# Pooling sums of keys and values by GpSimd, and batch 2 loaded in 72 rows, in a fused attention and feed-forward kernel

## Chip, cores, metric

One Trainium2 chip, one core. The time is the device time of one execution in microseconds (us); lower is better. Several executions are made of each kernel, and the medians below are of those. An execution is called slow when it is over 1.5% above the fastest of the same kernel; ratios and intervals use fast ones alone. Engines: PE is TensorE (matrix products; PEld its weight loads), DVE is VectorE, ACT is ScalarE, POOL is GpSimd, SP is SyncE, which here only issues loads and stores.

## The reference

Attention against keys and values that are averaged over groups of 8 positions, then a two-layer feed-forward with silu. All inputs and the output are float32.

```python
# q, k, v: (8 batches, 8 heads, 576 positions, 64); pool = 8, so Sp = 72
k_p = k.reshape(B, H, Sp, 8, D).mean(axis=3)
v_p = v.reshape(B, H, Sp, 8, D).mean(axis=3)
scores = (q @ k_p.T) / sqrt(D)
attn = exp(scores - max); attn /= sum(attn)
x = (attn @ v_p)  # -> (4608 tokens, 512)
# w_in: (512, 2048), w_out: (2048, 512)
h = x @ w_in
out = (h * sigmoid(h)) @ w_out
```

## The kernel before

The kernel goes through 9 tiles of 512 tokens (t = 0 to 8). Each tile has an "up" part (x times w_in, silu) and a "down" part (times w_out). From tile 1 on both are done with seven products of half size in place of eight (the Strassen-Winograd scheme): so DVE has to form sums such as `x_sum` (of quarters of x) and `h_sum` before TensorE can use them. The attention of batch t+1 is woven into tile t: a list of small pieces of work, the "fillers", each with the step of the up or down part at which it is put into the engines' instruction streams. An engine runs its stream in order: in experiment 2 below, TensorE stood for 1.9 us at the transposes of a late kp, and from 59 to 60 us it ran no product at all, though others stood behind them.

What the change touches is how the 8 positions of a group are summed. From batch 3 on, k and v come in by heads: 72 rows (one for each group) by 8 heads by 4 positions of 64. The first four positions are loaded by SP; the last four are *added* to them in flight by a load that POOL issues. That leaves four positions: `add_halves` makes two of them (72x1024 elements), `add_rest` one, in bf16. Batch 2 is done as batches 0 and 1 are: rows of 128 "slots" across heads, which TensorE must afterwards pick apart with selection products (`select_k`, `select_v`).

```python
def load_one(b, name):                       # first four positions, by SP
    raw = raw_tile(f"{name}_raw", H)
    load_rows(nc.sync, raw, source(b, name)[:, :, :PH])
    ...
def load_rest(b, name):                      # last four, added in flight
    nc.gpsimd.dma_start(out=batches[b][f"{name}_raw"],
        in_=source(b, name)[:, :, PH:], accum_op=ALU.add)

def add_halves(raw):
    nc.vector.tensor_add(out=raw[:, :, : 2 * D],
        in0=raw[:, :, : 2 * D], in1=raw[:, :, 2 * D :])
def add_rest(dst, raw):
    nc.vector.tensor_add(out=dst, in0=raw[:, :, :D]..., in1=raw[:, :, D : 2 * D]...)

def pool_k(b, stage):    # stage 0: add_halves; stage 1: add_rest twice, into kp
def pool_v(b):           # add_halves, add_rest into vp
def k_transpose(b):      # four products of 72x72: kp -> kT_ps, then ACT copies to kz

def unit_x_sum(t, n):    # both inputs lie in SBUF
    nc.vector.tensor_tensor(out=x_sum[:, U_XI[n]],
        in0=x_quarter(t, *a), in1=x_quarter(t, *b), op=...)

# up part, products "2", "5", "1" of a unit:
product(y, 2, "P", True); nc.scalar.copy(r_sb, ps["P"])
product(y, 5, "Q", True); tt(out=rr_sb, in0=ps["Q"], in1=r_sb, op=ALU.add)
product(y, 1, "R", True); tt(out=t_sb, in0=ps["R"], in1=rr_sb, op=ALU.subtract)

for t in range(NT):
    a = t + 1
    ...                                       # t >= 1:
    for n in U_X:                             # five x_sum, first in the up part
        f_up.append((0, lambda n=n: unit_x_sum(t, n)))
    ...
    elif t == 1:                              # batch 2, slots
        for j in range(2):
            f_up.append((0, lambda j=j: slot_sums("k", j, halves=True)))
            f_up.append((22, lambda j=j: select_k(2, j)))
            ...                               # copy_k, slot_sums of v, select_v, copy_v
    else:                                     # batches 3 to 7
        f_up.append((22, lambda: k_transpose(a)))
        f_down.append((10, lambda: pool_v(a)))
    ...
    elif a + 1 < B:
        for stage in range(2):
            f_down.append((100, lambda stage=stage: pool_k(a + 1, stage)))
        f_up.append((0, lambda: load_q(a + 1)))
        f_up.append((1, lambda: load_one(a + 1, "k")))
        f_up.append((2, lambda: load_rest(a + 1, "k")))
        f_down.append((11, lambda: load_one(a + 1, "v")))
        f_down.append((12, lambda: load_rest(a + 1, "v")))
```

The softmax here doesn't subtract the row's maximum and nothing guards it: scores larger than these inputs give would overflow.

## Time and profile before

| | before |
|---|---|
| time, median of the 3 runs made before the prediction (range) | 291.4 us (290.86 to 291.49) |
| span of the profiled execution | 288.6 us |
| busy: PE / DVE / ACT / POOL | 97% / 79% / 65% / 18% |
| granted PE clock, all 40 slices of the span | 0.9 or more |
| five x_sum of one tile, from first start to last end | 1.75 us |
| one 72x1024 add on DVE | 1.21 us |

The time is a little over the span, which is what the trace covers.

### The profile page before, as it was taken

The numbers are of one execution on the slowest core, as the hardware profiler recorded it, in microseconds if no ns is written. First come the engines' busy times: TensorE is split into PE (matmuls) and PEld (weight loads), VectorE is DVE, ScalarE is ACT, GpSimd is POOL, SyncE is SP. The second block draws the span as 40 slices with busy tenths as digits, with TensorE's granted clock in tenths as the row PEclk, the third lists the DMA queues.
The fourth block names the chain that finished last, engine by engine and source line by source line (L and its number), as shares of the span: only waits on it lengthen the run. The fifth ranks groups of instructions, "written<-read, shape, count | busy, mean of one in ns | idle before, by whom it ended". The sixth has DMA issues, their size and how long they took to land.

```text
span 288.6 us, 6600 instructions
## 1 busy us (share of the span) xinstructions
PE 281.2 (97%) x2578; PEld 189.9 (66%) x2597; DVE 226.8 (79%) x417; ACT 187.9 (65%) x401; POOL 52.2 (18%) x68
## 2 busy tenths in 40 slices
PE   7989999999999999999999999999999999999995
PEld 2448434465667676657788767676777667786684
DVE  4986844989789796979698879887988876746783
ACT  1768675568656877578767866786679657425700
POOL 8744316501020011101200106203000000000000
PEclk9999999999999999999999999999999999999999
DMA  7999999893758565875995495979830023005004
GB/s 214 276 278 215 232 301 151 221 206 55 145 82 187 127 91 76 133 179 123 137 182 166 61 138 81 164 156 163 149 82 2 2 65 83 1 2 140 6 2 145
DMA packets 35295, 37.67 MB, mean 131 GB/s; under 512 B 9952, under 2 KB 27616, under 8 KB 35264
## 3 DMA queue, kind: packets, MB, share of 16 engines
q0 software_dynamic: 21760, 20.86, 43.3%
q1 hardware_dynamic: 12928, 15.48, 22.0%
q10 hardware_dynamic: 576, 0.92, 0.9%
q8 instruction: 20, 0.33, 0.5%
q14 instruction: 11, 0.09, 0.1%
HBM read 36.70 MB, written 9.44 MB: 160 GB/s over the span
## 4 chain that ended last, share of the span: by engine, by line
PE 91%; DVE 2%; ACT 2%; DMA 2%; issue 1%; DVEq 0%
PE hp_ps L518 24%; PE o_psP L623 15%; PE o_psQ L623 15%; PE u_psQ L460 6%; PE u_psP L460 6%; PE o_psR L623 5%; PE o_ps L550 4%; PE sc_ps L330 4%; PE nu_ps L370 3%; PE den_ps L347 3%; PE u_psR L460 2%; DMA raw<-in_k_dram 2%; PE warm_ps L672 1%; ACT es L338 1%; PE kz_ps L295 1%
## 5 line engine op out<-in xcount | busy, mean ns | idle before, releaser
L518 PE MATMUL hp_ps<-xT,w_in_sb 128*128 128x512 bf16 (+3 forms) x398 | 80.5, 338 | 1.2 <-ACT h_T L524 0.4
L524 ACT ACTIVATE h_T<-hp_ps 128x512 bf16<-128x512 f32 (+2 forms) x95 | 51.4, 545 | 33.1 <-PE hp_ps L518 31.9
L623 PEld LDWEIGHTS <-h_sum 128*128 128x128 bf16 x640 | 60.4, 98 | 15.2 <-issue 6.1
L583 DVE TENSOR_TENSOR h_sum<-h_T 128x1024 bf16<-128x1024 bf16 (+1 forms) x72 | 50.9, 743 | 7.0 <-ACT h_T L524 7.0
L518 PEld LDWEIGHTS <-w_in_sb 128*128 128x128 bf16 x412 | 39.3, 98 | 24.9 <-issue 1.5
L338 ACT ACTIVATE es<-sc_ps 72x288 bf16<-72x288 f32 x128 | 41.4, 402 | 12.6 <-PE sc_ps L330 12.5
L378 DVE TENSOR_TENSOR xT<-nu_ps,rec 128x288 bf16<-128x288 f32 x64 | 25.8, 450 | 13.2 <-PE nu_ps L370 13.0
L460 PEld LDWEIGHTS <-w_sum 128*128 128x128 bf16 x300 | 29.3, 98 | 7.7
L623 PEld LDWEIGHTS <-h_T 128*128 128x128 bf16 x256 | 23.5, 98 | 6.7 <-issue 4.3
L468 ACT ACTIVATE h_T<-c_sb 128x512 bf16<-128x512 f32 x30 | 18.8, 628 | 10.8 <-DVE c_sb L492 10.8
L152 DVE STREAM_TRANSPOSE qT<-q_bf 128x576 bf16<-128x576 bf16 x32 | 22.9, 753 | 0.0
L181 POOL DMA_DIRECT2D raw<-in_k_dram x5 | 7.0, 1405 | 75.1 <-DVE h_sum L583 37.7
L356 ACT ACTIVATE lnd<-den_ps 128x288 f32<-128x288 f32 x30 | 12.3, 411 | 10.8 <-PE nu_ps L370 5.8
L273 DVE TENSOR_TENSOR raw<-raw 128x384 f32<-128x384 f32 (+3 forms) x20 | 12.4, 619 | 8.0 <-DMA raw<-in_v_dram 4.4
L623 PE MATMUL o_psP<-w_out_sb,h_sum 128*128 128x256 bf16 x128 | 17.6, 273 | 0.0
L623 PE MATMUL o_psQ<-w_out_sb,h_sum 128*128 128x256 bf16 x128 | 17.6, 273 | 0.0
L623 PE MATMUL o_psQ<-w_sum,h_T 128*128 128x256 bf16 x128 | 17.5, 274 | 0.0
L623 PE MATMUL o_psP<-w_sum,h_sum 128*128 128x256 bf16 x128 | 17.0, 273 | 0.0
L623 PE MATMUL o_psR<-w_sum,h_sum 128*128 128x256 bf16 x128 | 16.7, 273 | 0.0
L623 PE MATMUL o_psP<-w_sum,h_T 128*128 128x256 bf16 x128 | 16.7, 273 | 0.0
L530 POOL DMA_DIRECT2D out_dram<-o_sb x1 | 0.6, 628 | 82.3 <-issue 82.3
L623 PE MATMUL o_psQ<-w_sum,h_sum 128*128 128x256 bf16 x128 | 15.4, 273 | 0.0
(77 smaller groups left out, 426.8 us busy)
## 6 DMA issues: line engine op xcount, KB each, us to landing
out_dram<-o_sb SPq DMA_DIRECT2D x128, 64.0 KB, 2.5
q_bf<-in_q_dram POOLq DMA_DIRECT2D x6, 576.0 KB, 11.4
raw<-in_k_dram SPq DMA_DIRECT2D x6, 512.0 KB, 5.5
raw<-in_k_dram POOLq DMA_DIRECT2D x5, 576.0 KB, 8.8
raw<-in_v_dram POOLq DMA_DIRECT2D x5, 576.0 KB, 8.7
raw<-in_v_dram SPq DMA_DIRECT2D x5, 512.0 KB, 6.4
w_in_sb<-in_moe_w_in_dram POOLq DMA_DIRECT2D x8, 256.0 KB, 8.7
w_out_sb<-in_moe_w_out_dram POOLq DMA_DIRECT2D x4, 512.0 KB, 13.5
```

The costliest lines, as they stand in the source:

```text
L152: nc.vector.transpose(out=st["qT"][:, a, f * QF : (f + 1) * QF].rearrange("r i c p -> r (i c p)"), in_=st["q_bf"][:, a, f * n : (f + 1) * n],)
L273: nc.vector.tensor_add(out=raw[..., :w], in0=raw[..., :w], in1=raw[..., w : 2 * w])
L330: nc.tensor.matmul(sc[s], lhsT=kz[b % 2][rows, g, c, :], rhs=st["qT"][rows, g, f * QF : (f + 1) * QF, c, :], start=(c == 0), stop=(c == 1),)
L338: nc.scalar.activation(es[:, s, :], sc[s], func=AF.Exp, scale=score_scale)
L356: nc.scalar.activation(lnd, den_ps[:, :HS], func=AF.Ln)
L378: nc.vector.tensor_mul(out=xT[:, 2 * g + c, cols], in0=nu[c][:, :HS], in1=rec)
L460: nc.tensor.matmul(ps[bank][:, u, :], lhsT=w[:, kk, 128 * u : 128 * (u + 1)], rhs=x[:, kk, :], start=first and u == 0 and kk == 0, stop=kk ...
L468: nc.scalar.activation(h_T[:, g : g + 2, j * NQ : (j + 1) * NQ], src, func=AF.Silu)
L518: nc.tensor.matmul(hp_ps[:, r0:r1], lhsT=w_in_sb[:, kk, g * 128 : (g + 1) * 128], rhs=xT[:, kk, x0 : x0 + r1 - r0], start=(kk == 0), stop= ...
L524: nc.scalar.activation(h_T[:, g, n0 : n0 + n], hp_ps[:, :n], func=AF.Silu)
L583: nc.vector.tensor_tensor(out=h_sum[n][:, ks, :], in0=quarter(*a, ks), in1=quarter(*b, ks), op=op)
L623: nc.tensor.matmul(ps[b][:, c, :], lhsT=left(n, kt, c), rhs=W_OUT[n][:, kt, :], start=b not in begun, stop=kt == k1 - 1, skip_group_check= ...
```

## The change

Intent: DVE is busy for 79% of the span and POOL for 18%, so the sums of batches 3 to 7 (19.3 us of DVE) go to POOL. Batch 2 is loaded by heads like the later batches, which also does away with its selection products on TensorE. The loads of v now follow those of k at once. All sums of batch 2 on are made by POOL, in POOL's stream, where they stand behind its loads.

```diff
-    def load_one(b, name):
+    def load_one(b, name, eng=nc.sync):
...                                         # POOL's form: one load of 72 rows
     def add_halves(raw):
-        nc.vector.tensor_add(
+        nc.gpsimd.tensor_add(
...
     def add_rest(dst, raw):
-        nc.vector.tensor_add(
+        nc.gpsimd.tensor_add(
...
-            elif t == 1:
-                for j in range(2):
-                    f_up.append((0, lambda j=j: slot_sums("k", j, halves=True)))
-                    f_up.append((22, lambda j=j: select_k(2, j)))
...                                         # copy_k, slot_sums("v"), select_v, copy_v
             else:
                 f_up.append((22, lambda: k_transpose(a)))
-                f_down.append((10, lambda: pool_v(a)))
...
             if t == 0:
-                f_down.append((0, lambda: load_half_2("k", 0)))
+                f_down.append((0, lambda: load_one(2, "k", nc.gpsimd)))
                 f_down.append((0, lambda: load_q(2)))
-                f_down.append((0, lambda: load_half_2("k", 1)))
-                for half in range(2):
-                    f_down.append((31, lambda half=half: load_half_2("v", half)))
+                f_down.append((0, lambda: load_rest(2, "k")))
+                f_down.append((31, lambda: load_one(2, "v", nc.gpsimd)))
+                f_down.append((31, lambda: pool_k(2)))
+                f_down.append((31, lambda: load_rest(2, "v")))
...
             elif a + 1 < B:
-                for stage in range(2):
-                    f_down.append((100, lambda stage=stage: pool_k(a + 1, stage)))
                 f_up.append((0, lambda: load_q(a + 1)))
+                if t == 1:
+                    f_up.append((0, lambda: pool_v(2)))
                 f_up.append((1, lambda: load_one(a + 1, "k")))
+                f_up.append((1, lambda: load_one(a + 1, "v")))
                 f_up.append((2, lambda: load_rest(a + 1, "k")))
-                f_down.append((11, lambda: load_one(a + 1, "v")))
-                f_down.append((12, lambda: load_rest(a + 1, "v")))
+                f_up.append((2, lambda: load_rest(a + 1, "v")))
+                f_down.append((30, lambda: pool_k(a + 1)))
+                f_down.append((31, lambda: pool_v(a + 1)))
```

(Cuts are marked with "..."; the helpers of the slot loads lose their "halves" form.)

More of the change, by code (lines that the diff above doesn't have):

```diff
@@ L172, in load_rows @@
             eng.dma_start(out=out[r0:r1], in_=in_[r0:r1])
-    def load_one(b, name):
+    def load_one(b, name, eng=nc.sync):
         st = batches.setdefault(b, {})
         raw = raw_tile(f"{name}_raw", H)
-        load_rows(nc.sync, raw, source(b, name)[:, :, :PH])
+        if eng is nc.sync:
+            load_rows(eng, raw, source(b, name)[:, :, :PH])
+        else:
+            eng.dma_start(out=raw, in_=source(b, name)[:, :, :PH])
         st[f"{name}_raw"] = raw
@@ L196, in add_rest, with pool_k @@
         )
-    def pool_k(b, stage):
+    def pool_k(b):
         st = batches[b]
         raw = st["k_raw"]
-        if stage == 0:
-            add_halves(raw)
-            return
+        add_halves(raw)
         st["kp"] = mid.tile([SP, 2, 2, 4, DH], BF16, tag="kp", bufs=1, name="kp")
@@ L247, with load_slots @@
     }
-    def load_slots(eng, b, name, i0, i1, half=None):
-        es = slice(0, RE) if half is None else slice(half * RE // 2, (half + 1) * RE // 2)
+    def load_slots(eng, b, name, i0, i1):
         src = (k if name == "k" else v)[b].rearrange("h (sp p) d -> (h sp) (p d)", p=POOL)
-        src = src[:, es]
-        how = dict(accum_op=ALU.add) if half else {}
         tiles = row_tiles[name]
-        w = es.stop - es.start
         if i0 == SLOTS:
-            eng.dma_start(
-                out=tiles[1][:REST, SLOTS - SA, :w], in_=src[128 * SLOTS :], **how
-            )
+            eng.dma_start(out=tiles[1][:REST, SLOTS - SA], in_=src[128 * SLOTS :])
         else:
@@ L263, in load_slots, with slot_sums @@
             eng.dma_start(
-                out=tiles[j][:, i0 - SA * j : i1 - SA * j, :w],
-                in_=src[128 * i0 : 128 * i1].rearrange("(i r) e -> r i e", r=128), **how
+                out=tiles[j][:, i0 - SA * j : i1 - SA * j],
+                in_=src[128 * i0 : 128 * i1].rearrange("(i r) e -> r i e", r=128),
             )
-    def slot_sums(name, j, halves=False):
+    def slot_sums(name, j):
         raw = row_tiles[name][j]
         dst = rows5[name][:, SA:] if j else rows5[name][:, :SA]
-        w = RE // 4 if halves else RE // 2
+        w = RE // 2
         while w > D:
@@ L750 @@
     load_w_out(3)
-    def load_half_2(name, half):
-        for i0, i1 in ((0, SA), (SA, SLOTS), (SLOTS, SLOTS + 1)):
-            load_slots(nc.gpsimd, 2, name, i0, i1, half)
     visits = [(f, g) for f in range(2) for g in range(2)]
@@ L809 @@
                     f_down.append((37 + 3 * j, lambda j=j: copy_v(1, j)))
-            elif t == 1:
-                for j in range(2):
-                    f_up.append((0, lambda j=j: slot_sums("k", j, halves=True)))
-                    f_up.append((22, lambda j=j: select_k(2, j)))
-                    f_up.append((23, lambda j=j: copy_k(2, j)))
-                    f_down.append((8, lambda j=j: slot_sums("v", j, halves=True)))
-                    f_down.append((40, lambda j=j: select_v(2, j, "at")))
-                    f_down.append((41, lambda j=j: copy_v(2, j)))
             else:
                 f_up.append((22, lambda: k_transpose(a)))
-                f_down.append((10, lambda: pool_v(a)))
             for n in range(4):
```

## The prediction

> **What bounds the kernel now.** I read the page first: the busy shares, then the chain that ended last.
>
> ```profile
> PE 281.2 (97%) x2578; PEld 189.9 (66%) x2597; DVE 226.8 (79%) x417; ACT 187.9 (65%) x401; POOL 52.2 (18%) x68
> ...
> PE 91%; DVE 2%; ACT 2%; DMA 2%; issue 1%; DVEq 0%
> ```
>
> TensorE is 91% of the chain; DVE is 2% of it (about 6 us), although it is 79% busy. So taking work off DVE pays only where DVE is on the chain, and POOL is nearly idle: its 52 us are almost all DMA issues. I then followed the chain in order of time, tile by tile of 512 tokens. In the middle of the kernel (tile 2, "up" part) it leaves TensorE once:
>
> ```profile
> 91.47 0.45 PE u_psP L460 x4
> 91.92 0.04 DVEq L492
> 91.95 0.45 DVE qT L152 x2
> 92.40 0.14 issue
> 92.54 0.66 DVE c_sb L492
> 93.20 0.02 issue
> 93.23 0.02 ACT h_T L468
> 93.25 0.51 issue
> 93.76 0.58 ACT r_sb L477
> 94.34 0.02 issue
> 94.36 0.70 DVE rr_sb L480
> 95.07 0.04 issue
> 95.11 0.60 PE u_psQ L460 x4
> ```
>
> (Columns: start, length, engine and line.) DVE reaches c_sb late because three query transposes, and ahead of them x_sum, stand in its queue; ACT and TensorE then wait in turn. The same detour is at 122 us (tile 3) and nowhere in tiles 4 to 6, where the chain is TensorE throughout. What is it worth? The chain's groups give 0.865 us for four 512-wide products of hp_ps and 0.44 us for four of u_ps. An up part of tile 2 has 32 of the first and 14 groups of the second: 8 x 0.865 + 14 x 0.44 = 13.1 us, with 0.13 us of kT_ps 13.2. The measured up part runs from 85.68 to about 99.17, 13.5 us. Loss: 0.3 us. Tile 3 is the same. In the down parts the chain never leaves TensorE.
>
> Batch 2 is used in tile 1. There the chain, 50 to 87 us, has selection products that the change deletes:
>
> ```profile
> 58.58 0.22 PE hp_ps L518
> 58.80 0.67 PE kz_ps L295 x16
> 59.47 0.16 issue
> ...
> 73.88 0.53 PE v_ps L313 x12
> ```
>
> [...] For DVE this trace has 1212 ns for the 72x1024 add[...]; for GpSimd it has no add at all. [...] every second half is issued by POOLq. So the accumulating loads and the new adds share one in-order queue.
>
> **The change part by part.**
>
> *Removed from TensorE.* 24 k selections (0.67 + 0.16 us of the chain, 0.83) and 12 v selections (0.53); added are four transposes of 72x72, 0.13 us as in the other tiles. Net 0.83 + 0.53 - 0.13 = 1.2 us, all on the chain, so a saving if kp and vp are there in time.
>
> *Removed from DVE.* From the groups by shape:
>
> ```profile
> L187 DVE TENSOR_TENSOR raw<-raw 72x1024 f32<-72x1024 f32 x10 | 12.1, 1212 | 0.0
> ...
> L192 DVE TENSOR_TENSOR kp<-raw 72x256 bf16<-72x256 f32 x10 | 3.8, 418 | 0.2
> ...
> L192 DVE TENSOR_TENSOR vp<-raw 72x512 bf16<-72x512 f32 x5 | 3.4, 687 | 0.2
> ```
>
> That is 19.3 us for batches 3 to 7. For batch 2: the slot sums, 2 x (556 + 358 + 423 + 291) ns = 3.3 us, and the copies out of PSUM, 2 x 303 + 2 x 417 ns = 1.4 us. Together 24 us, of 226.8, so DVE should show about 203 us busy. On the chain it is worth little. The sums of k at the end of each down part (2.0 us of DVE just before x_sum) go away, so x_sum and rr_sb come earlier. In tiles 2 and 3 this can remove the detour: 2 x 0.3 = 0.6 us. Elsewhere nothing.
>
> *Added to POOL.* [...] POOL has room; what matters is when kp lands.
>
> *Moved.* Both first halves are now issued after the stores of the tile before, v no longer in the middle of the down part, and the second halves follow on. TensorE's queue is in order: if kp is late, it stands at kT_ps. So I set the time of kp against that of kT_ps. The DMA figures are of before:
>
> ```profile
> raw<-in_k_dram SPq DMA_DIRECT2D x6, 512.0 KB, 5.5
> raw<-in_k_dram POOLq DMA_DIRECT2D x5, 576.0 KB, 8.8
> ```
>
> (last column: us from issue to landing). Issue times are from POOL's and SP's order of time in before.
> - Batch 2: first half issued at 30 us, landed at 44 (the queue is full of weights), second half 8 us more, 52; sums to 56; kT_ps is due at 58.6. Slack 2.5 us.
> - Batches 3, 4 and 6: the second halves land about 78, 111 and 172, so kp is ready at 82, 115 and 176, against 90.7, 120.8 and 180.0. Slack 4 us or more.
> - Batch 5: SP is busy with stores until 127.9; second half issued at 135.1, 9 to 10 us beside v, 144.5; kp at 148 to 149 against 150.3. Slack 1 to 2 us.
> - Batch 7: stores until 188.4, second half issued at 194.9, landed 204.5 as it now runs beside that of v; kp at 208 to 209 against 209.6. Slack about 1 us.
> Before, DVE did these last two sums at 144.3 and 203.5 in 2.0 us; the 1.6 us more on POOL come from what slack there was. vp is due only at 46 of 112 steps of the down part, over 10 us later than kT_ps, so v has room everywhere; in tile 4 its buffer is still read by the deferred numerator of batch 4, which delays pool_v(6) to about 166, and that is harmless too.
>
> The sum without delays: 291.4 - 1.2 - 0.6 = 289.6 us. For delays I take expected values: 0.3 us at batch 2, 0.4 at batch 5, 0.6 at batch 7. I choose these from slacks of 1 to 2.5 us [...]. [...] Predicted: 289.6 + 1.5 = 291.1 us.
>
> **The rivals.**
> 1. *A wait for POOL takes the place of the work.* If an add takes 1.5 to 2 times my estimate, pool_k is 5.5 to 7 us, and kp comes 1 us late for batch 5, 1 to 3 for batch 7, up to 1 for batch 2. TensorE then stands at kT_ps for 3 to 5 us in all: 293 to 295 us. For it: the slacks above[...]. Against it: four of six batches have slack enough.
> 2. [...] h_sum or x_sum (two SBUF inputs) wait, and everything behind them in DVE's order, among it the evacuations that free the PSUM banks. 12 long adds at 0.3 us on the chain make 3 to 4 us: 293 us. For it: 64 h_sum, 40 x_sum and 30 weight sums are of that kind, and batches 5 and 7 would be summed just when x_sum is due. Against it: each place where POOL might block DVE has 2 us less of DVE work in front of it than before, and an evacuation has about 1.7 us (the next product of 16) to spare.
> 3. *All goes well.* kp is early everywhere, and the detours vanish: 289.3 to 289.8 us. For it: POOL idles for 82 us at the end, and waits of over 10 us stand before its second halves. Against it: batch 7.
> 4. *POOL's order delays loads.* An add that waits for its data holds back the queries and second halves behind it, so that the delay grows from batch to batch. Against it: each batch starts afresh behind SP's stores, and queries are loaded two buffers ahead. I give it little.
>
> **Range and chances.** The gain is bounded at about 2 us, 0.7%, because the removed DVE work lies beside TensorE; faster by 2% would need 5.8 us, which nothing in the chain offers. Slower by 2% (297.2) needs stalls of over 7.6 us, that is, adds of over twice the estimate or DVE blocked widely. The low end is 289.2, the third rival; the high end 294.5, the first rival or the second nearly in full. Chances: faster 0.02, same 0.86, slower 0.12.
>
> **What would show it.** Right: DVE about 203 us busy, POOL about 90, a 72x1024 add on POOL near 2.3 us, no v_ps or kz_ps products after tile 0, tile 1 shorter by over 1 us, the chain in tiles 2 and 3 without the 122 us detour. For the first rival: waits of PEld L221 for POOL kp, of over 0.5 us, foremost in tiles 4 and 6. For the second: h_sum or x_sum well over their 685 and 416 ns while POOL adds, and waits of TensorE for DVE. I am wrong if POOL's adds take 4 us or more, if vp holds up the numerators, or if time is lost in tile 0, where the loads of batch 2 change.

## More of the kernel before

The five x_sum stand at the boundary of two tiles, and the sums of k just ahead of them. This is DVE's order of time at the boundary of tiles 2 and 3, before (columns: start, length of the group, engine and line, operation, out<-in, shapes, count):

```profile
115.04 1.21 DVE L187 TENSOR_TENSOR raw<-raw 72x1024 f32<-72x1024 f32 x1
116.29 0.76 DVE L192 TENSOR_TENSOR kp<-raw 72x256 bf16<-72x256 f32 x2
...
117.57 1.75 DVE L427 TENSOR_TENSOR x_sum<-xT 128x512 bf16<-128x512 bf16 x5
119.24 0.68 DVE L480 TENSOR_TENSOR rr_sb<-u_psQ,r_sb 128x512 f32<-128x512 f32 x1
```

Tile 3 starts at 115.61 (its first product of the up part), so rr_sb, for which TensorE will come to wait in the changed kernel, starts 3.6 us into the tile.

## The result

| | median | range | fast runs against before |
|---|---|---|---|
| before (a fourth run added) | 291.28 us | 290.86 to 291.49 | |
| changed | 300.22 us | 297.16 to 302.75 | 1.0272 [1.0212, 1.0332], slower |

A ratio compares the fast runs of one kernel with the fast runs of the other from the same rounds, so it is not quite the ratio of the medians; in brackets is the 95% interval. A kernel is called slower or faster from 2% on, and "same" below. The 291.1 us predicted is 9 us too low, and the range ended at 294.5. The changed kernel also spreads more (297 to 303 us) than the one before (0.2%).

The profile of that first result fell in a slow execution (302.75 us). So the changed kernel was run again, and the lines below are of that repeat, whose profiled execution is a fast one (299.55 us, span 297.7, against 288.6 before). First the page: busy times, granted PE clock in 40 slices, and the shares of the chain that ended last.

```profile
PE 284.4 (96%) x2565; PEld 190.0 (64%) x2565; DVE 216.0 (73%) x380; ACT 188.7 (63%) x402; POOL 97.0 (33%) x90
...
PEclk9999999999999999979999999999999999999999
...
PE 69%; DMA 13%; DVE 6%; issue 6%; POOL 5%; ACT 0%; POOLq 0%; DVEq 0%
```

DVE has lost 37 instructions but only 11 us of busy time; POOL has gained 45 us; TensorE has 32 weight loads fewer (2565 against 2597), yet is busy 3 us longer, and its clock has a dent in the 18th slice (126 to 134 us: 7 tenths, 9 in all others). The 13% of DMA in the chain are no measure of the loss: the four long loads on it all lie before 56 us, where the chain, once it has left TensorE at a wait for POOL, is followed back through the first loads; the kernel of experiment 6, as fast as before, also has 13%. Next, what TensorE stood waiting for (total us, times, longest):

```profile
PE u_psQ L455 <- DVE rr_sb L475: 5.4, 3, 3.7
...
PE nu_ps L365 <- POOL vp L195: 1.4, 1, 1.4
...
PE kT_ps L222 <- POOL kp L195: 0.7, 2, 0.4
```

In the trace before, the longest wait of a TensorE product on another engine, after the warm-up, is 0.4 us. The waits for kp and vp were foreseen in kind (the prediction's first rival) and are small. The large one is for rr_sb, on DVE. Why is rr_sb late? DVE's order of time at the boundary of tiles 2 and 3, after:

```profile
119.13 6.77 DVE L422 TENSOR_TENSOR x_sum<-xT 128x512 bf16<-128x512 bf16 x5
125.82 0.68 DVE L475 TENSOR_TENSOR rr_sb<-u_psQ,r_sb 128x512 f32<-128x512 f32 x1
```

and POOL's in the same stretch:

```profile
117.65 2.35 POOL L190 TENSOR_TENSOR raw<-raw 72x1024 f32<-72x1024 f32 x1 [6.45 <-DMA raw<-in_k_dram]
120.08 1.65 POOL L195 TENSOR_TENSOR kp<-raw 72x256 bf16<-72x256 f32 x2
121.69 2.52 POOL L190 TENSOR_TENSOR raw<-raw 72x1024 f32<-72x1024 f32 x1
124.29 1.32 POOL L195 TENSOR_TENSOR vp<-raw 72x512 bf16<-72x512 f32 x1
```

The five x_sum, 1.75 us before, take 6.77 us, exactly while POOL makes the sums of k and v of batch 4. Taken apart into single instructions from the trace's records, the two engines interlock one by one:

| POOL instruction | ends at | x_sum | starts, length | ends at |
|---|---|---|---|---|
| 72x1024 add of k | 120.00 | 1st | 119.13, 1.15 | 120.28 |
| kp, first half | 120.86 | 2nd | 120.20, 0.94 | 121.15 |
| kp, second half | 121.73 | 3rd | 121.07, 0.94 | 122.01 |
| 72x1024 add of v | 124.21 | 4th | 121.94, 2.56 | 124.49 |
| vp | 125.61 | 5th | 124.42, 1.48 | 125.90 |

Each x_sum ends 0.28 or 0.29 us after the end of a POOL instruction: it waits for the whole of it, gets one turn, and by then the next POOL instruction has the lead over the next x_sum. Five additions of 0.42 us each pay for five additions of POOL. rr_sb stands behind them and starts 7.5 us into the tile (125.82 - 118.32), in place of 3.6.

It does not end there. The engines' busy times in 2 us windows (columns: window, length, busy us and count for PE, PEld, DVE, ACT, POOL; granted PE clock; DMA share; GB/s):

```profile
124.00:126.00 2.00, 0.00 (x0) 0.00 (x0) 2.00 (x3) 0.00 (x0) 1.92 (x3) 1.00 0.60 138
...
128.00:130.00 2.00, 2.00 (x11) 1.44 (x10) 1.87 (x3) 0.76 (x3) 0.00 (x0) 0.50 1.02 175
130.00:132.00 2.00, 2.00 (x13) 1.47 (x12) 1.03 (x2) 1.65 (x3) 0.00 (x0) 0.66 1.08 257
```

TensorE is idle for 3.7 us, and soon after it is back its clock is granted at 0.50 and 0.66 for 4 us (0.99 in the 2 us before them, 1.00 in the 2 us after). The work lost to that is 2 x 0.50 + 2 x 0.34 = 1.7 us. In the chain of the changed kernel the groups of four u_ps products take 0.85 us in this stretch, where they take 0.44 us else.

Where the 9.1 us of span went, by tile (length from the first up product of a tile to that of the next, us; tile 0 from the start of the span):

| tile | 0 | 1 | 2 | 3 | 4 | 5 | 6 |
|---|---|---|---|---|---|---|---|
| before | 53.50 | 32.02 | 30.09 | 29.64 | 29.84 | 29.54 | 30.00 |
| changed (fast repeat) | 53.86 | 33.25 | 31.21 | 34.85 | 29.62 | 30.72 | 30.00 |
| five x_sum in it, changed | none | 1.76 | 4.01 | 6.77 | 1.75 | 3.73 | 1.76 |

Tile 0 took 53.50 to 54.16 us in kernels whose tile 0 is the same (before, and experiments 3, 4, 5 and 10 below), so 0.4 us there is no finding. Tiles 2, 3 and 5 lose 7.5 us together, and they are the ones whose x_sum are stretched; tile 1, where batch 2 is used, loses 1.2 though its TensorE work shrank. So there were two things to explain, and they suggested four theories:

- **Exclusion theory (mine after the result):** POOL's two-input additions and DVE's exclude each other, and it is the x_sum on TensorE's path that pay. The cost sits in the *moment* at which POOL adds, not in the amount of its work.
- **Load theory:** the new loads (v's next to k's, 72-row form, issued by POOL) land late, and that is what delays things.
- **POOL too slow:** kp and vp come late because POOL needs 7.4 us a batch, undisturbed, where DVE needed 3.9.
- **Batch 2 theory:** the new form of batch 2 is what costs, and all later delays are its echo.

### The profile page after: what moved, and what is told of

Its sections match the earlier page's. It is cut to its first block, busy times and chain, and to the rows that moved or that the text cites.

```text
span 300.9 us, 6532 instructions
## 1 busy us (share of the span) xinstructions
PE 285.3 (95%) x2565; PEld 190.3 (63%) x2565; DVE 217.5 (72%) x380; ACT 188.7 (63%) x402; POOL 96.5 (32%) x90
## 4 chain that ended last, share of the span: by engine, by line
PE 64%; DMA 13%; issue 8%; DVE 7%; POOL 6%; ACT 0%; POOLq 0%; DVEq 0%
PE o_psP L618 14%; PE o_psQ L618 14%; PE hp_ps L513 13%; PE u_psQ L455 6%; PE u_psP L455 5%; DVE x_sum L422 5%; DMA w_out_sb<-in_moe_w_out_dram 5%; PE o_psR L618 4%; DMA w_in_sb<-in_moe_w_in_dram 3%; DMA raw<-in_k_dram 3%; POOL raw L190 3%; PE sc_ps L325 3%; DMA raw<-in_v_dram 2%; PE nu_ps L365 2%; PE den_ps L342 2%
## 5 line engine op out<-in xcount | busy, mean ns | idle before, releaser
L513 PE MATMUL hp_ps<-xT,w_in_sb 128*128 128x512 bf16 (+3 forms) x412 | 82.8, 340 | 0.4 <-ACT h_T L519 0.4
L513 PEld LDWEIGHTS <-w_in_sb 128*128 128x128 bf16 x412 | 39.3, 98 | 24.9 <-issue 1.5
L190 POOL TENSOR_TENSOR raw<-raw 72x1024 f32<-72x1024 f32 x12 | 32.5, 2706 | 38.8 <-DMA raw<-in_k_dram 25.0
L455 PEld LDWEIGHTS <-w_sum 128*128 128x128 bf16 x300 | 30.1, 100 | 8.5 <-issue 0.3
L184 POOL DMA_DIRECT2D raw<-in_k_dram x6 | 8.5, 1418 | 55.4 <-DMA raw<-in_k_dram 39.0
L422 DVE TENSOR_TENSOR x_sum<-xT 128x512 bf16<-128x512 bf16 x40 | 24.7, 682 | 0.0
L455 PEld LDWEIGHTS <-w_in_sb 128*128 128x128 bf16 x120 | 11.7, 97 | 12.2 <-issue 8.3
L351 ACT ACTIVATE lnd<-den_ps 128x288 f32<-128x288 f32 x30 | 12.3, 411 | 10.2 <-PE nu_ps L365 5.8
```

The costliest lines, as they stand in the source:

```text
L190: nc.gpsimd.tensor_add(out=raw[:, :, : 2 * D], in0=raw[:, :, : 2 * D], in1=raw[:, :, 2 * D :])
L351: nc.scalar.activation(lnd, den_ps[:, :HS], func=AF.Ln)
L422: nc.vector.tensor_tensor(out=x_sum[:, U_XI[n]], in0=x_quarter(t, *a), in1=x_quarter(t, *b), op=ALU.subtract if n in (3, 4) else ALU.add,)
L455: nc.tensor.matmul(ps[bank][:, u, :], lhsT=w[:, kk, 128 * u : 128 * (u + 1)], rhs=x[:, kk, :], start=first and u == 0 and kk == 0, stop=kk ...
L513: nc.tensor.matmul(hp_ps[:, r0:r1], lhsT=w_in_sb[:, kk, g * 128 : (g + 1) * 128], rhs=xT[:, kk, x0 : x0 + r1 - r0], start=(kk == 0), stop= ...
```

## The experiments

All twelve kernels gave correct results. Times are medians; the kernel before ran beside each of them, at 290.8 to 291.3 us. By the 2% rule only experiments 1 and 4 are "slower" and all others "same"; what is said of smaller differences rests on the 95% intervals of the ratios.

### 1. The changed kernel again

No edit; it gives the fast profile used above, and a base beside the runs of the two parts.

> The changed kernel again, for a profile in the fast state beside the next three on one chip. Theory A ([...]each DVE add with two SBUF inputs waits for the POOL add in front of it, and x_sum at the start of an up part is the victim): 297 to 301 us, some of tiles 2, 3 and 5 with five x_sums in 3.5 to 7.2 us instead of 1.75, TensorE waiting for rr_sb. Theory B (lateness: the 72-row loads of batch 2 and the slower POOL sums make kp and vp late): the same time, but the larger part of the loss at kT_ps and nu_ps.

Measured: 299.85 us (299.36 to 304.18 with one slow run), 1.0299 [1.0264, 1.0333]. The loss is real and reproducible. The total of the x_sum in the three worst tiles was 3.76, 7.17 and 5.02 us in the slow profile and 4.01, 6.77 and 3.73 in this one: how the two engines meet varies from run to run, which fits the larger spread of this kernel.

### 2 and 3. The two parts of the change apart

Batch 2 alone: its loads by heads, no selections, all sums on DVE (those of batch 2 at step 20 of the up part of tile 1).

```diff
-                for j in range(2):
-                    f_up.append((0, lambda j=j: slot_sums("k", j, halves=True)))
...
+                for stage in range(2):
+                    f_up.append((20, lambda stage=stage: pool_k(2, stage)))
+                f_up.append((22, lambda: k_transpose(2)))
+                f_down.append((10, lambda: pool_v(2)))
```

> Batch 2 loaded in 72 rows with DMA accumulation and summed on DVE, without selections; batches 3 to 7 exactly as before. Theory A: no POOL adds, so no x_sum delay; only the lateness of batch 2 stays: kT_ps 1 us late less 1.2 us of selections saved, 290 to 292 us. Theory B: the late loads are the loss, 295 us or more.

POOL sums alone: batch 2 in slots as before, batches 3 to 7 summed by POOL. From batch 4 on the loads of v also follow those of k at once, as in the change, so this is the POOL sums together with those loads.

```diff
     def add_halves(raw):
-        nc.vector.tensor_add(
+        nc.gpsimd.tensor_add(
...                                         # add_rest likewise
+                v_to, v_at = (f_down, 11) if t == 1 else (f_up, 1)
+                v_to.append((v_at, lambda: load_one(a + 1, "v")))
...                                         # loads and sums placed as in the change
```

> POOL sums for batches 3 to 7 as changed; batch 2 in slots with selections as before. Theory A: tile 1 as before (32 us), x_sums still stretched in tiles where the adds fall at the start of the up part: 294 to 299 us. Theory B: about 291 to 293 us, as batch 2 is in time again.

| | median | against before |
|---|---|---|
| batch 2 alone | 293.41 us | 1.0081 [1.0051, 1.0112] |
| POOL sums alone | 294.53 us | 1.0122 [1.0082, 1.0161] |
| both (experiment 1) | 299.85 us | 1.0299 [1.0264, 1.0333] |

Each part loses by itself, 2.6 and 3.7 us, and together they lose 9.0: more than the sum. (Batch 2 alone fell between its two expectations, 290 to 292 us and 295 or more.) In the POOL kernel the x_sum of tiles 3, 5 and 6 took 4.32, 3.80 and 2.83 us, without batch 2 being touched: so the batch 2 theory can't be the whole. Its order of time shows why it loses less. POOL's first add in front of tile 3 starts at 111.93, 3.7 us before the tile does, so only the last two POOL instructions meet the x_sum:

```profile
111.93 2.35 POOL L187 TENSOR_TENSOR raw<-raw 72x1024 f32<-72x1024 f32 x1 [4.41 <-DMA raw<-in_k_dram]
...
115.73 2.34 POOL L187 TENSOR_TENSOR raw<-raw 72x1024 f32<-72x1024 f32 x1
118.15 1.33 POOL L192 TENSOR_TENSOR vp<-raw 72x512 bf16<-72x512 f32 x1
```

With both parts it starts only 0.7 us before the tile, because its data are later: the second half of k(4) is issued at 107.86 in place of 102.64. That delay began at batch 2 (experiment 12 looks at it). The waits of POOL alone were at most 1.0 us each, and TensorE's mean granted clock was 1.000 over this execution.

In the batch 2 kernel TensorE stood once for kp, for 1.9 us, and then ran at a reduced clock (granted 0.63 from 62 to 64 us and 0.52 from 64 to 66, 1.00 before and after):

```profile
PE kT_ps L224 <- DVE kp L195: 1.9, 1, 1.9
```

DVE's order of time there, though, shows no wait for the data (the second half of k had landed at 54.14); the sum simply stood behind rr_sb in DVE's stream, where I had put it at step 20, and began at 59.14:

```profile
58.53 0.69 DVE L483 TENSOR_TENSOR rr_sb<-u_psQ,r_sb 128x512 f32<-128x512 f32 x1 [2.42 <-ACT r_sb L480]
```

DVE was idle for 2.42 us just before. So this kernel's loss is in part my own making, and experiment 9 mends it.

### 4. POOL additions of idle data, on top of the kernel before

To part POOL's adding as such from all else: everything of the kernel before stays, and POOL adds, in tiles 2 to 6, the same shapes on a tile of zeros that nothing reads, released at the last store copy but one of the tile before. Its loads of q are put ahead.

```diff
+    def idle_adds(src):
+        nc.gpsimd.tensor_copy(out=gate, in_=src)        # waits for src
+        big_add()                                       # 72x1024 f32
+        for n in range(2):
+            nc.gpsimd.tensor_add(out=idle_b[:SP, :256], ...)
+        big_add()
+        nc.gpsimd.tensor_add(out=idle_b[:SP], ...)      # 72x512
...
+            if 2 <= t <= 6:
+                f_up.append((-1, lambda: idle_adds(o_sb[0][:, 0, :1])))
...
-                f_up.append((0, lambda: load_q(a + 1)))
+                f_up.append((-2, lambda: load_q(a + 1)))
```

> The kernel before, plus on POOL five adds on scratch data of the changed kernel's sizes (72x1024, 2 of 72x256, 72x1024, 72x512; 8.7 us) in each of tiles 2 to 6, released just before x_sum. No data of the kernel depends on them. Theory A: x_sums 5 to 7 us instead of 1.75 in all five tiles, TensorE waits 2 to 5 us in each: 301 to 315 us. Theory B: within 1 us of before, 291 to 292 us.

Measured: 304.27 us, 1.0459 [1.0427, 1.0491]. Additions whose results nobody reads cost 13 us: neither new data nor POOL's results can be the cause, only POOL's being active then. (POOL's loads stood behind these additions, but in tiles 2 to 6 neither DVE nor TensorE waited for a load.) Which DVE instruction paid was not what I had thought. At the start of tile 3:

```profile
118.75 3.00 DVE L194 TENSOR_TENSOR kp<-raw 72x256 bf16<-72x256 f32 x2
...
122.28 1.75 DVE L429 TENSOR_TENSOR x_sum<-xT 128x512 bf16<-128x512 bf16 x5
```

```profile
118.73 1.88 POOL L762 TENSOR_TENSOR idle<-idle 72x1024 f32<-72x1024 f32 x1
...
122.42 3.36 POOL L762 TENSOR_TENSOR idle<-idle 72x1024 f32<-72x1024 f32 x1
```

(DVE first, POOL second.) Here the kp sums, still on DVE and ahead of the x_sum, were the ones to wait (0.76 us became 3.00), and they pushed the x_sum back; the x_sum themselves were undisturbed. POOL's second big add then took 3.36 us in place of 1.88: it started 0.14 us after the first x_sum and ended at 125.78, 1.75 us after the last of the five (124.03). So it, too, made hardly any way until all five were through: the exclusion goes both ways.

### 5. The same idle additions, released by the last x_sum

```diff
+            if 2 <= t <= 6:
+                f_up.append((0, lambda: idle_adds(x_sum[:, 4, 1, :1])))
```

> The same idle POOL adds as in r4, same number and sizes, but released behind the fifth x_sum of tiles 2 to 6, where DVE's next two-SBUF-input work (h_sum) comes some 6 to 8 us later. Theory A (a DVE op with two SBUF inputs waits for the POOL add in front): nearly free, 291 to 294 us, the DVE sum of k and x_sum at their old lengths. Rival (POOL adds cost wherever they lie, by SBUF or instruction traffic, or through the in-order POOL queue and its loads): 300 us or more, as in r4.

Measured: 295.59 us, 1.0144 [1.0127, 1.0161]. From +13.4 us to +4.3 by moving the same additions by a few us. In tiles 2, 3 and 6 it cost nothing visible (30.14, 29.68 and 30.02 us against 30.09, 29.64 and 30.00), tile 4 lost 0.6 (there DVE's sum of k waited 0.8 us for a load that POOL had issued later). What is left sits in tile 5 (33.27 us against 29.54): there POOL first had eight loads of q for the last batch to issue, so the copy ahead of its additions began 10.2 us into the tile, in place of 3.8 as in tile 3, and the additions met h_sum, which also has two inputs in SBUF:

```profile
186.17 4.06 DVE L585 TENSOR_TENSOR h_sum<-h_T 128x1024 bf16<-128x1024 bf16 x2
```

Two h_sum take 1.29 us undisturbed. TensorE then waited 2.0 us for h_sum. The time missed the expectation of 291 to 294 us, but 3.7 of the 4.3 us lost are in tile 5, where the same overlap struck in another place.

### 6. The changed kernel with its sums released behind x_sum

Batches 3 to 7: a one-column copy that reads the last x_sum stands ahead of POOL's sums; loads of q come first, and k_transpose goes from step 22 to 38 of the up part, as kp is now later. Batch 2 stays as changed.

```diff
+    def behind_x_sum():
+        nc.gpsimd.tensor_copy(out=gate, in_=x_sum[:, 4, 1, :1])
...
-                f_up.append((22, lambda: k_transpose(a)))
+                f_up.append((22 if t == 1 else 38, lambda: k_transpose(a)))
+            if t >= 2:
+                f_up.append((0, lambda: behind_x_sum()))
+                f_up.append((0, lambda: pool_k(a)))
+                f_up.append((0, lambda: pool_v(a)))
...
-                f_down.append((30, lambda: pool_k(a + 1)))
-                f_down.append((31, lambda: pool_v(a + 1)))
```

> The changed kernel with the POOL sums of batches 3 to 7 released behind x_sum of the tile that uses them, and kT_ps at step 38 of the up part instead of 22; batch 2 as changed. Theory A: tiles 2 to 6 as long as before or up to 0.4 us shorter, tile 1 still 1 to 3 us longer: 291 to 294 us. If the loss of tiles 2, 3 and 5 came from late data, summing still later makes it worse: 300 us or more.

Measured: 291.26 us over 12 runs, 1.0003 [0.9986, 1.0020]: 8.6 us came back. POOL does the same sums (96.1 us busy against 97.0). The x_sum of tiles 2 to 6 took 1.75 us again, tiles 2 and 3 are now *shorter* than before (29.77 and 29.29 us against 30.09 and 29.64), and what DVE does beside most of POOL's additions is not stretched; these have at most one input in SBUF (POOL's first add of tile 3, then DVE's transposes and c_sb, which run beside it, the kp sums and the next add; they took 2.09 and 0.65 us in the kernel before):

```profile
119.78 2.34 POOL L190 TENSOR_TENSOR raw<-raw 72x1024 f32<-72x1024 f32 x1
```

```profile
121.44 2.08 DVE L152 STREAM_TRANSPOSE qT<-q_bf 128x576 bf16<-128x576 bf16 x3
123.45 0.65 DVE L487 TENSOR_TENSOR c_sb<-u_psP,t_sb 128x512 f32<-128x512 f32 x1
```

Only the last of POOL's sums, vp, still meets two h_sum (1.75 us in tile 3, undisturbed 1.29), and TensorE doesn't wait for these. So neither the slowness of POOL nor late loads of batches 3 to 7 were the cause: POOL takes as long here, and the second half of k(4) is issued at 105.90, in the changed kernel at 107.86. The later step of k_transpose can't explain the gain either, as TensorE had waited 0.7 us in all for kp, in tile 1. What still costs is tile 1 (32.85 us, 0.8 above before), where batch 2's sums meet the x_sum (4.99 us for the five) and h_sum.

### 7 and 8. Are batch 2's loads at fault?

Both start from the batch 2 kernel (experiment 2). In 7 its loads are split into 64 and 8 rows, as SP's are; in 8 its first halves are issued by SP.

```diff
-            eng.dma_start(out=raw, in_=source(b, name)[:, :, :PH])
+            load_rows(eng, raw, source(b, name)[:, :, :PH])
```

> r2 (batch 2 in 72 rows, DVE sums) with each of its four loads split in 64 and 8 rows. If the shape of 72 rows makes these loads slow, k's second half lands 3 us or more earlier, the wait at kT_ps (2 us in r2) goes, and the time is 289.5 to 290.5 us. If it is the order of the two halves (the second waits for the first, and little is in flight meanwhile), it stays at 292 to 294 us.

```diff
-                f_down.append((0, lambda: load_one(2, "k", nc.gpsimd)))
+                f_down.append((0, lambda: load_one(2, "k")))
...
-                f_down.append((31, lambda: load_one(2, "v", nc.gpsimd)))
+                f_down.append((0, lambda: load_one(2, "v")))
```

> r2 with the first halves of batch 2 issued from SP, which is idle then, so that they do not queue behind the weights on POOL's queue; both at once at the start of the down part of tile 0. If queueing behind the weights is the cause of the lateness: the first half of k lands before 42 us instead of 46, kp is in time, 289.5 to 291 us, unless the weights come late in exchange (waits of o_ps in tile 0). If the accumulating second half is the slow part: 292 to 294 us.

Measured: 292.74 us, 1.0066 [1.0039, 1.0094], and 293.53 us, 1.0076 [1.0054, 1.0099], against 293.41 us, 1.0081, of experiment 2. Tile 1 took 35.02 us in both, 34.89 in experiment 2. Neither helps, and neither made the second half of k land earlier: at 54.72 and 55.17, in experiment 2 at 54.14. In all three it was there over 4 us before DVE began its sum, so the loads are not what TensorE waits for at batch 2; experiment 9 tests the place of the sum. (What these loads do to SP's stores is told under experiment 12.)

### 9. Batch 2 alone, its sum right behind x_sum

One number of experiment 2 is changed:

```diff
-                    f_up.append((20, lambda stage=stage: pool_k(2, stage)))
+                    f_up.append((0, lambda stage=stage: pool_k(2, stage)))
```

> r2 with the DVE sum of k of batch 2 right behind x_sum in DVE's order instead of behind rr_sb. In r2, r7 and r8 alike DVE began it at 59.1 to 59.6 us without waiting for a load, so the loss there is ascribed to its place, not to the loads. Expected: kp ready near 58.5 us, no wait at kT_ps, tile 1 30.8 us (32.0 less 1.2 of selections), 289.5 to 290.5 us. If the loads were the cause: DVE waits there for the second half and it stays at 292 to 294 us.

Measured: 291.06 us over 14 runs, 0.9998 [0.9986, 1.0009]. DVE makes kp in the gap in which it had stood idle, at 56.95 us in place of 59.14, and TensorE no longer waits. Tile 1 fell from 34.89 to 30.95 us, which is 1.07 below the kernel before: this is the saving by the deleted selection products, and the prediction had 1.2. The whole time missed the expected 289.5 to 290.5 us, and the gain does not show in it: in this profile tiles 0 and 6 were 1.0 and 0.3 us longer. Experiment 2, with the same loads in tile 0, had 53.62 us there, this one 54.54; whether that is scatter or a cost of the new loads stays open.

### 10. POOL sums alone, released behind x_sum

Experiment 3 with the release of experiment 6 (loads of q first and k_transpose at step 38 too); batch 2 as before.

```diff
+                f_up.append((0, lambda: behind_x_sum()))
+                f_up.append((0, lambda: pool_k(a)))
+                f_up.append((0, lambda: pool_v(a)))
```

> r3 (POOL sums for batches 3 to 7, batch 2 in slots) with the sums released behind x_sum, as in r6. Theory A: the 3.7 us of r3 go, and the detours of tiles 2 and 3 too (0.3 us each): 290 to 290.8 us.

Measured: 290.17 us over 14 runs, 0.9968 [0.9958, 0.9978], against 1.0122 without the release. All x_sum take 1.75 to 1.77 us for five. The intent of the change was sound: in tiles 2 and 3 the chain no longer leaves TensorE. The stretch in which the prediction found a detour over DVE and ACT now reads:

```profile
120.91 0.86 PE hp_ps L516 x4
121.77 0.44 PE u_psP L458 x4
122.21 0.44 PE u_psQ L458 x4
```

These tiles take 29.80 and 29.30 us, 0.3 less each.

### 11. Both parts, repaired

POOL sums of batches 3 to 7 released behind x_sum (10), batch 2 by heads but summed by DVE right behind x_sum (9). The loads of v(3) are back in the down part, as before the change.

```diff
+        eng = nc.vector if b == 2 else nc.gpsimd
...
+                if t == 1:
+                    f_up.append((0, lambda: pool_k(2)))
+                    f_down.append((10, lambda: pool_v(2)))
```

> All of the change but with both repairs: batch 2 in 72 rows summed on DVE behind x_sum, batches 3 to 7 summed on POOL behind x_sum. Theory A: 1.2 us of selections and 0.6 us of detours saved, none of the waits: 289 to 290 us, faster than before by 0.4 to 0.7%.

Measured: 289.37 us, 0.9942 [0.9919, 0.9965], the fastest kernel: 1.6 us below before and 10.5 below the changed one. All 40 x_sum of the kernel took 415 to 424 ns (410 to 2556 in the changed one; columns: minimum, median, maximum in ns, then first and last start in us):

```profile
L424 DVE TENSOR_TENSOR x_sum<-xT x40: 415/418/424, 55.1 to 260.9; 128x512 bf16<-128x512 bf16 x40
```

Tiles 1, 2 and 3 took 30.95, 29.75 and 29.30 us: 1.07, 0.34 and 0.34 below before, and TensorE is 94% of the chain. From experiment 10 to this one batch 2's new form brings 0.8 us.

### 12. The changed kernel, batch 2's sums alone moved to DVE

Does batch 2's place in POOL's stream cause the delays further on? POOL sums of batches 3 to 7 stay unreleased, as changed. The edit also puts the loads of v(3) back into the down part, as before, so it is not batch 2's sums alone.

```diff
-                f_down.append((31, lambda: pool_k(2)))
...
-                    f_up.append((0, lambda: pool_v(2)))
+                    f_up.append((0, lambda: pool_k(2)))
+                    f_down.append((10, lambda: pool_v(2)))
...                                         # v(3): steps 11 and 12 of the down part
```

> The changed kernel with only batch 2 summed on DVE (k behind x_sum, v where it was); POOL sums of batches 3 to 7 where the change has them. It tells what POOL's sums of batch 2 alone cost. If the two parts simply add up: r3's 294.5 less 1.2, 293 to 294 us, so that POOL's sums of batch 2 cost 6 us, partly by making the later sums fall on x_sum. If it is 297 us or more, the POOL sums of batches 3 to 7 are the loss by themselves.

Measured: 295.54 us (294.23 to 299.06, one run slow), 1.0139 [1.0103, 1.0174], where the changed kernel had 1.0299: 4.7 us less by these ratios. It is more than the 293 to 294 us of parts that simply add up, and less than 297. Tile 1 alone gives 33.25 - 30.95 = 2.3 of the 4.7, taking the 30.95 us of experiment 11, whose tile 1 has the same batch 2. The profile fell in the slow execution, so its times are not compared with fast ones; but within it x_sum took 6.31 us in tile 3 and 6.20 in tile 5, against 2.82 in tile 2 and 1.75 undisturbed. So the loss at x_sum remains without batch 2 on POOL; the batch 2 theory falls as the sole cause.

Does it aggravate? In the changed kernel POOL's add of v(2) was itself blocked by a run of DVE's two-input additions (four w_sum and four h_sum back to back, to 72.79 us), and POOL's second half of k(3) stood behind it:

```profile
68.87 6.12 POOL L190 TENSOR_TENSOR raw<-raw 72x1024 f32<-72x1024 f32 x1 [6.72 <-PE hp_ps L513]
...
77.15 1.40 POOL L184 DMA_DIRECT2D raw<-in_k_dram  x1
```

In the POOL kernel of experiment 3 that last load is issued at 68.63. But at most 2.1 of these 8.5 us can be POOL's: the first half of k(3), to which this one is added, landed only at 75.06 (67.53 in experiment 3), because SP issued it behind its sixteen stores of tile 0, and these took twice as long. SP's order of time in experiment 3, then in the changed kernel:

```profile
49.22 9.36 SPq L536 DMA_DIRECT2D out_dram<-o_sb  x16
58.76 1.56 SPq L172 DMA_DIRECT2D raw<-in_k_dram  x2
```

```profile
49.39 17.32 SPq L533 DMA_DIRECT2D out_dram<-o_sb  x16
66.89 1.28 SPq L172 DMA_DIRECT2D raw<-in_k_dram  x2
```

The stores ended at 57.8 to 58.9 us in the five kernels with batch 2 in slots, at 61.4 and 61.6 in experiments 7 and 8, and at 64.7 to 66.8 in the others with batch 2 by heads (67.6 in this slow profile), wherever it is summed. So the load theory is right in one thing: batch 2's new loads go along with later stores, and these with a later k(3). Where the sums are released behind x_sum it costs little: experiment 11, the fastest kernel, has it too (66.8). That this delay pushed the sums of later batches onto the x_sum fits the times of issue, but no run moved it alone.

## Why the prediction was wrong

**What was right.** The duration of POOL's additions: near 2.3 us predicted for 72x1024, though no trace then held an addition on POOL; 2.35 measured undisturbed (for a batch 2 x 2.35 + 2 x 0.72 + 1.27 = 7.4). POOL's busy time: about 90 predicted, 97.0 measured. The saving by the selections: 1.2 predicted, 1.07 in tile 1 of experiments 9 and 11. The detours of tiles 2 and 3: 0.3 us each predicted, 0.29 to 0.34 in experiments 10 and 11. The sum without delays, 289.6 us, is close to what the repaired kernel needs (289.37; a saving of 1.6 us against 1.8 predicted). The delays expected for late data were 1.3 us in sum and wrongly placed: at batch 2, 0.3 us expected, 0.7 for kp and 1.4 for vp measured; at batches 5 and 7, 0.4 and 0.6 expected and no wait for kp measured. The sum, 2.1, is a small part of the loss.

**The step that failed** is the smallest term of the 1.5 us added to 289.6: beside the 1.3 for late data, 0.2 us for DVE's additions that wait while POOL adds. It was mis-sized: tiles 2, 3 and 5 lose 7.5 us in the fast profile, and moving POOL's sums of batches 3 to 7 behind x_sum (experiment 6) brings 8.6 us back. That h_sum or x_sum would wait was named, as the second rival, but for x_sum with the sums of batches 5 and 7; those of 3, 4 and 6 struck (tiles 2, 3 and 5), and those of 5 and 7 did not (1.75 and 1.76 us for the x_sum of tiles 4 and 6). Its argument against was that "each place where POOL might block DVE has 2 us less of DVE work in front of it than before". Three things were missing in that.

1. *The unit of the loss.* I counted one block of 0.3 us for each long add. The 0.3 us was my estimate; no trace then showed the two engines adding at once. In the fast profile an x_sum of 0.42 us that came while POOL was adding waited until the whole POOL instruction was through (the longest took 2.56 us), and the five x_sum met five of them in turn: 5 us in tile 3, against the 2 us of slack that I had set against it.
2. *The coincidence.* I set kp's arrival against kT_ps only (is it late?), and had the sums of batches 5 and 7 close to x_sum, those of 3, 4 and 6 early. I did not ask for each what DVE is doing when POOL *starts*. Nor did I ask whether the times of issue of before would stand: the second halves of k for batches 3, 4 and 6, which I had landing at 78, 111 and 172 us, landed at 86.8, 117.6 and 178.2. Batch 4's kp, which I had ready at 115, was made from 117.65 on, and POOL's sums of that batch ran to 125.6 and hit tile 3 fully.
3. *The clock.* A 3.7 us wait was followed by 4 us at 0.50 and 0.66 of the clock, which cost 1.7 us more. No step of mine had that.

DVE's busy time shows the same error from another side: 203 us predicted, 216.0 measured. 9.3 us of the difference is the x_sum alone (mean 646 ns, before 416): the time in which x_sum waits for POOL is counted in its busy time. A reader who looks only at busy shares sees DVE relieved, from 79% to 73%, while it had become what TensorE waits for.

**Of the rivals.** A wait for POOL in place of the work (the first) was real but 2.1 us in the waits view. POOL's order delaying loads (the fourth), to which I gave little, did happen at batch 2, but by at most 2.1 us through POOL; the larger part of k(3)'s delay came by way of SP's stores (experiment 12). "All goes well" was what the idea can give when POOL is released at the right moment.

**What stays open.** Who of two waiting instructions comes next: in tile 3 the engines took turns, while in tile 1, and in experiment 4, POOL waited for the whole run of DVE's additions. The runs show both patterns, and not what decides between them. Also open are why experiment 9's gain in tile 1 is not in its total, why the stores of tile 0 take longer beside batch 2's new loads, and how much of the 9.0 us comes from the two parts striking together.

## What to carry to other kernels

Before moving work from DVE to GpSimd, don't look at DVE's busy share; list DVE's instructions with two inputs in SBUF that stand on the path to TensorE, and ask where GpSimd's additions will fall among them: here each of the five x_sum of tile 3, 0.42 us undisturbed, took 0.94 to 2.56 us, as it waited for a GpSimd instruction. If there is a stretch in which DVE reads PSUM or has one SBUF input (here c_sb and the transposes, 0.65 and 2.08 us beside GpSimd's additions, 0.65 and 2.09 without), tie GpSimd's work to its start with a small dependency; here that one-column copy (0.18 us on POOL) turned +3.7 us into -0.8 us. And an instruction moved in an in-order stream needs its place checked against what stands ahead of it, as the sum behind rr_sb showed (2.4 us from experiment 2 to 9).

## What the traces showed of the engines

- DVE's additions with both inputs in SBUF were stretched beside POOL's additions; the transposes and the additions that read PSUM were not (2.08 us for three transposes and 0.65 for c_sb in experiment 6, 2.09 and 0.65 in the kernel before). A *series* cost more than one block: five x_sum of 0.42 us met five POOL instructions one by one, 1.75 us becoming 6.77; and a run of eight DVE additions, to 72.79 us, held one POOL addition until 74.99, 2.35 us becoming 6.12. Which engine follows when both have the next instruction waiting is not shown: both patterns occurred here.
- The waiting was counted as busy time of the waiting engine: the mean of x_sum went from 416 to 646 ns with no idle time in front of it, so busy time was no measure of work done.
- POOL's 72x1024 f32 addition took 2.35 us undisturbed. The sum in place on one and the same tile (experiment 4, both inputs the same) took 1.88 us.
- TensorE's clock was lowered after the long wait (3.7 us idle, then 0.50 and 0.66 over 4 us). After shorter waits it sometimes was as well, and sometimes not. Waits of 1.9 to 2.0 us were followed by it in experiment 2 (for kp; 0.63 and 0.52 over 4 us), once in 4 (for h_sum; 0.50 at 200 to 203 us), and, by the length of the products, in 7 and 8 (for kp; four u_ps products took up to 1.06 us, undisturbed 0.60). After one of 2.0 us in experiment 5 (for h_sum) and three of 1.8 to 1.9 us in experiment 4 (for x_sum) the products kept their lengths. So here a wait of 2 us may or may not have cost clock; what decides is not shown by these runs. In the three fast profiles whose clock was read (experiments 1, 2 and 4) the lowered stretch cost 1.7 us each time, the sum of the missing clock over its windows.
